# Masks of four score pairs written by ScalarE into PSUM, and a new written order for the first phase of a band-attention and feed-forward kernel

## The chip, the cores and the metric

The kernel runs on one core of one Trainium2 chip. A core has five engines, each with an instruction queue of its own that it works off strictly in order: TensorE (PE; matmuls, with weight loads shown apart as PEld), VectorE (DVE), ScalarE (ACT), GpSimd (POOL) and SyncE (SP), which only issues transfers here. ACT and POOL issue transfers too. TensorE writes its results into PSUM, eight banks of 128 x 512 fp32 numbers; DVE and ACT can read and write PSUM.

The metric is the device time of the kernel in microseconds, the median of the runs.

## The reference, cut to what matters

The inputs are q, k and v for 8 batches of 8 heads, 576 positions and 64 numbers per head, and two weight matrices, w_in of 512 x 2048 and w_out of 2048 x 512. What is computed:

```
scores = q @ k.T / sqrt(64)
mask   = (rel >= 0) & (rel < 64)            # rel = query position - key position
attn   = softmax(where(mask, scores, -1e9))
x      = (attn @ v) as 4608 rows of 512      # 8 heads side by side
h      = x @ w_in
out    = max(0.01 * h, h) @ w_out
```

All of it is fp32.

## The kernel before, in words

**Attention.** A query block of 64 positions sees only its own 64 keys and the 64 before. Two such query blocks make a pair m, 36 pairs in all; a pair's scores fill two PSUM banks (j = 0 and 1), with number b = 2m + j. So one bank is 128 keys x 512 (four head pairs, two query blocks, 64 queries). The mask is added in PSUM: before the score matmuls, one matmul of a unit matrix with the mask pattern (0 or a large negative number) writes the whole bank, and the scores then accumulate on it. Softmax runs over the 128 partitions: POOL takes the maximum over them, DVE subtracts it, ACT takes the exponential, and the sum comes out of the value matmul through a column of ones beside v.

**Feed-forward.** fp32 weights and activations are split into a high and a low part of a faster format (fp32r in the profile), and each product is three matmuls. The weights arrive as 64-bit numbers in 32 raw blocks (w_in and w_out by turns), and DVE and ACT turn each into fp32 and then into the two parts.

**Stages.** The 4608 rows are 9 chunks of 512. A first phase does attention for pairs 0 to 7 (chunks 0 and 1) and most of the feed-forward products of these chunks, while the weights are converted. It follows a list written out by hand, ORDER (line 54): every name in it is one step, the list is walked once, and each engine's queue gets its instructions in just this order. What stands behind the bar in ORDER, and all later stages (the rest of the attention, then products for the other chunks that use seven in place of eight block products), is ordered by a planner with fixed costs; the planner does not look at the first phase.

The steps of ORDER, by their letters, with the engine and the line of the profile:

| step | what it does | engine, line |
|---|---|---|
| q, k, v (number m) | loads of a pair | SP, 163, 167, 174 |
| raw n | loads weight block n (n < 3 on SP, else on ACT) into one of three buffers | 210 |
| bits, sign, clamp, join, rest n | conversion of weight block n | DVE, 225, 229, 237, 242, 251 |
| abs, chi n | conversion of weight block n; chi also stores the block of w_in | ACT, 233, 245 |
| X n | n idle matmuls on zeros | PE, 503 |
| S m | mask matmuls (312) and score matmuls (278) of pair m | PE |
| Z b | mask of pair 0, added behind its scores | PE, 312 |
| E b | scores out of PSUM: b < 2 on DVE (322), else on ACT (324) | |
| P b | maximum over the partitions | POOL, 332 |
| N b | subtracts the maximum by a matmul in the bank, b < 4 | PE, 346 |
| sub b | subtracts the maximum, b from 4 | DVE, 337 |
| exp b | exponential | ACT, 351, 353 |
| V b | values | PE, 367 |
| sm, rec, y b | sum, its inverse, the product | DVE, 374, 379, 386 |
| T m | transposes the pair's result into a PSUM bank | PE, 393 |
| H m, L m | high and low part of x | ACT 397, DVE 401 |
| M k | first product of job k, 12 matmuls | PE, 431 |
| lk, gh, gl k | leaky ReLU and the two parts of its result | ACT 436, 441, DVE 445 |
| W k | second product of job k | PE, 467 |
| ev | an accumulated bank out of PSUM | ACT, 476 |

Jobs 0 to 5 take half of chunk 0 each (256 columns; jobs 0 to 2 need x of pairs 0 and 1, jobs 3 to 5 of pairs 2 and 3), jobs 6 to 10 the whole of chunk 0, jobs 11 to 18 chunk 1. M k needs the L of its pairs and the rest of its weight block; W k needs gl k.

The banks: scores of pairs 1 and 3 use two banks of one pool (tags o0, o1); those of the other pairs use tags s and t, and so does T from pair 2 on (tag s). T of pairs 0 and 1 uses tag o3.

Of the kernel before, what the change touches and what calls it, by code (L numbers as in the profile page):

```python
# [60 lines left out]
E9 S5 v5 q6 k6 raw8 lk3 gh3 chi5 abs6 sub8 bits7 exp8 gl3 M4 lk4 rest5 sign7 clamp6 W2 V8 P9 abs7 sub9 join6 gh4 raw9  # L61
M5 bits8 gl4 E10 sm8 sign8 exp9 chi6 W3 P10 clamp7 rec8 y8 join7 rest6 lk5 abs8 clamp8 gh5 V9 M6 W4 gl5 join8 bits9
sub10 sm9 sign9 rec9 y9 raw10 E11 raw11 chi7 P11 chi8 lk6 exp10 T4 gh6 abs9 rest8 rest7 bits10 M7 V10 W5 gl6 sign10
clamp9 H4 abs10 sub11 join9 L4 bits11 sm10 rec10 clamp10 y10 join10 lk7 raw12 exp11 gh7 gl7 S6 V11 chi9 rest9 sign11
# [40 lines left out]
def band_attention_ffn(ctx: ExitStack, tc: tile.TileContext, qk, vW, vL, w_in, w_out, eye_mask, out, outT):  # L105
# [159 lines left out]

    def quarter_scores(m, ps, begun, more=False):

        q = q_of(m)  # L270
# [1156 lines left out]
```

## Time and profile before

| what | value |
|---|---|
| median of three runs | 850.16 us (849.91 to 851.41) |
| the profiled execution's own time | 850.4 us |
| its span, first to last instruction | 848.6 us |
| PE busy | 841.8 us, 99% |
| weight loads busy | 686.3 us, 81% |
| DVE busy | 620.1 us, 73% |
| ACT busy | 375.7 us, 44% |
| POOL busy | 383.3 us, 45% |
| data moved | 226.80 MB, 267 GB/s over the span |

An engine's busy time is the union of its instructions' times. Matmuls are pipelined, and their ends are modelled in the profile, so a matmul's own duration is longer than the step to the next one; the steps tell what a matmul costs. The same holds, less so, for DVE and ACT: an instruction's duration reaches a little into the next one.

The first phase goes to about 128.65 us, where the first product behind ORDER starts (line 920).

### The profile page before, as it was taken

The page shows a single profiled execution, that of the slowest core. Times are in us where ns is not written, and L with a number is a line of the kernel's source. Part 1 is how long each engine was busy: PE and PEld are TensorE (multiplying, and loading weights), DVE is VectorE, ACT ScalarE, POOL GpSimd, SP SyncE. Part 2 cuts the span into 40 slices and gives each one's busy share as a digit, 9 for nine tenths or more (in the row PEclk, how much of TensorE's full clock was granted, in tenths as well). Part 3 has the DMA queues.
Part 4 walks back from the last instruction along what each step waited for, and adds up shares of the span by engine and source line. Part 5 has one row for each costly group of instructions (what it writes and reads, how often), then busy time and mean ns, then how long its engine had stood idle before and what let it go on. Part 6 is the DMA issues. An engine that isn't in the chain of part 4 may idle for free.

```text
span 848.6 us, 16788 instructions
## 1 busy us (share of the span) xinstructions
PE 841.8 (99%) x6778; PEld 686.3 (81%) x6778; DVE 620.1 (73%) x883; ACT 375.7 (44%) x605; POOL 383.3 (45%) x218
## 2 busy tenths in 40 slices
...
GB/s 324 273 233 155 253 162 235 264 284 271 288 307 323 301 212 286 314 305 317 333 351 358 365 351 318 365 310 311 242 272 235 238 248 196 198 198 198 193 211 92
DMA packets 127757, 226.80 MB, mean 267 GB/s; under 512 B 15552, under 2 KB 46400, under 8 KB 127680
## 3 DMA queue, kind: packets, MB, share of 16 engines
...
## 4 chain that ended last, share of the span: by engine, by line
PE 97%; DVE 2%; DMA 0%; ACT 0%; issue 0%; ACTq 0%
PE m L1118 27%; PE z L1181 18%; PE acc L929 11%; PE h L920 11%; PE y L1138 10%; PE h L431 5%; PE acc L467 5%; PE s L278 4%; PE o L740 4%; PE o L367 1%; DMA qk<-qk 0%; PE t L393 0%; DVE raw L225 0%; PE s L312 0%; DVE w L242 0%; DVE raw L229 0%
## 5 line engine op out<-in xcount | busy, mean ns | idle before, releaser
L1118 PE MATMUL m<-pfew,p 128*128 128x512 f32 x720 | 169.4, 391 | 0.0
L1118 PEld LDWEIGHTS m<-pfew,p 128*128 128x128 f32 x720 | 134.5, 188 | 28.3
L1102 POOL DMA_DIRECT2D p<-w_first x42 | 31.8, 757 | 113.4 <-PE m L1118 61.0
L929 PE MATMUL acc<-p,gs 128*128 128x512 f32 x324 | 80.6, 394 | 0.0
L1127 DVE TENSOR_TENSOR p<-m,pxa 128x512 f32<-128x512 f32 x60 | 41.3, 689 | 47.0 <-PE m L1118 46.0
L681 POOL PARTITION_ALL_REDUCE g<-late_f x20 | 36.8, 1875 | 78.7 <-DVE late_f L666 72.0
L684 POOL PARTITION_ALL_REDUCE late_o<-late_f x20 | 66.1, 3329 | 12.2 <-ACT late_f L692 7.0
L1118 PE MATMUL m<-pxb,p 128*128 128x512 f32 x288 | 70.9, 391 | 0.0
L1130 ACT ACTIVATE p<-p 128x512 f32<-128x512 f32 x60 | 37.9, 631 | 73.6 <-DVE p L1127 73.5
L929 PEld LDWEIGHTS acc<-p,gs 128*128 128x128 f32 x324 | 59.8, 188 | 12.8
L1127 DVE TENSOR_TENSOR pxa<-m,pxa 128x512 f32<-128x512 f32 x60 | 41.4, 690 | 35.4 <-PE m L1118 34.7
L684 POOL PARTITION_ALL_REDUCE late_o<-e x18 | 59.5, 3336 | 8.5 <-ACT e L692 3.6
L1118 PEld LDWEIGHTS m<-pxb,p 128*128 128x128 f32 x288 | 53.7, 188 | 11.3
L684 POOL PARTITION_ALL_REDUCE late_o<-late_e x18 | 59.3, 3322 | 5.5 <-ACT late_e L692 5.2
L1181 PE MATMUL z<-gs,p 128*128 128x512 f32 x240 | 57.6, 389 | 0.0
L920 PE MATMUL h<-pxa,p 128*128 128x512 f32 x228 | 54.9, 390 | 0.0
L1102 POOL DMA_DIRECT2D p<-w_second x28 | 22.7, 811 | 68.5 <-PE z L1181 31.0
L1181 PEld LDWEIGHTS z<-gs,p 128*128 128x128 f32 x240 | 45.0, 188 | 9.4
L1181 PE MATMUL z<-third,p 128*128 128x512 f32 x216 | 51.9, 389 | 0.0
L1181 PE MATMUL z<-pxa,p 128*128 128x512 f32 x216 | 51.9, 389 | 0.0
L920 PEld LDWEIGHTS h<-pxa,p 128*128 128x128 f32 x228 | 42.7, 188 | 9.0
L1102 POOL DMA_DIRECT2D p<-w_sums x16 | 12.0, 747 | 80.2 <-PE z L1181 55.8
...
## 6 DMA issues: line engine op xcount, KB each, us to landing
...
```

Of the source, the lines that this page charges most:

```text
L431: nc.tensor.matmul(ps, a[:, k, :], b[:, k, part], start=n == 0, stop=n == len(terms) - 1)
L467: nc.tensor.matmul(acc[c, i], a[:, ts], b, start=begin and n == 0, stop=end and n == 2)
L681: nc.gpsimd.partition_all_reduce(most_of(j), e_of(m)[:, j], P, ReduceOp.max)
L684: nc.gpsimd.partition_all_reduce(sum_of(j), e_of(m)[:, j], P, ReduceOp.add)
L920: nc.tensor.matmul(ps, a[:, k, :], b[:, k], start=i == 0, stop=i == len(terms) - 1)
L929: nc.tensor.matmul(acc[c, i], a[:, i * P : (i + 1) * P], b, start=begin and k == 0, stop=n in ends and k == 2)
L1102: nc.gpsimd.dma_start(to, of, max_dma_last_dim=2048)
L1118: nc.tensor.matmul(tiles[b], w[:, 256 * i + 128 * kt : 256 * i + 128 * kt + 128], x_part(OF_X[k], j, kt), start=begin and c == 0, stop=c = ...
L1127: nc.vector.tensor_tensor(to(), tiles[b], x(), ALU.add)
L1130: nc.scalar.activation(to(), to() if b is None else tiles[b], AF.Prelu, alpha=0.01)
L1138: nc.tensor.matmul(tiles[i], a, b, start=f == 0 and k == 0, stop=f == FT - 1 and k == 2)
L1181: nc.tensor.matmul(tiles[b + i], a, x, start=begin and f == 0 and c == 0, stop=f == half - 1 and c == 2, skip_group_check=not begin,)
```

## The change

Six of the mask matmuls go from PE to ACT. For pairs 4 and 5 (both banks) and 6 and 7 (bank j = 1), a new step A m copies the mask pattern from SBUF into the bank with ScalarE, ahead of the score matmuls, which accumulate on it as they did on the mask matmul's result. Bank j = 0 of pairs 6 and 7 keeps its mask matmul. T of pairs 2 and 3 now uses tag o3 and no longer a score bank. And the whole list of the first phase, ahead of the bar, is replaced by another one with the same steps and the four steps A4 to A7; the list behind the bar is the same.

```diff
+SEEDED, TURNED_OVER = 4, 6
 ORDER = """
-q0 X6 S0 k1 raw0 q1 E0 P0 E1 bits0 sign0 raw1 v0 q2 k2 P1 X3 Z0 Z1 S1 abs0 E2 N0 exp0 X1 N1 bits1 sign1 abs1 clamp0
-join0 clamp1 V0 sm0 join1 exp1 V1 E3 S2 chi0 raw2 chi1 raw3 rec0 sm1 rec1 bits2 sign2 y1 y0 P2 P3 N2 raw4 E4 rest1
-rest0 E5 exp2 N3 exp3 T0 v1 V2 V3 k3 q3 abs2 H0 S3 v2 v3 q4 k4 sm2 P4 sub4 P5 rec2 sm3 L0 y2 rec3 clamp2 y3 exp4 V4 E6
-T1 join2 H1 sub5 sm4 bits3 rec4 L1 exp5 X4 V5 P6 raw5 chi2 sign3 abs3 E7 bits4 rest2 sub6 sm5 clamp3 rec5 y4 y5 sign4
-P7 M0 lk0 exp6 gh0 M1 abs4 gl0 T2 W0 join3 sub7 bits5 clamp4 V6 lk1 H2 exp7 raw6 L2 gh1 join4 V7 S4 chi4 raw7 chi3 gl1
-sm6 sign5 sm7 rest4 rec7 rec6 rest3 M2 E8 abs5 y7 y6 T3 bits6 sign6 W1 lk2 H3 L3 clamp5 P8 M3 gh2 gl2 join5 v4 k5 q5
...
-sign15 chi14 E15 exp14 chi13 abs15 lk9 gh9 P15 rec13 y13 V14 T6 rest14 rest13 sub15 M10 sm14 clamp15 gl9 rec14 join15
-y14 exp15 raw17 H6 chi15 V15 W9 bits16 sign16 L6 lk10 gh10 abs16 raw18 sm15 rec15 gl10 y15 T7 H7 rest15 W10 clamp16
-bits17 join16 sign17 L7 abs17 clamp17 join17 bits18 raw19 chi16 ev0 chi17 ev1 raw20 rest16 sign18 abs18 rest17 M11
...
-gh17 bits27 clamp26 gl17 sign27 join26 abs27 clamp27 join27 chi26 lk18 chi27 gh18 bits28 sign28 rest26 gl18 k8 q8 v8
-W17 q9
+q0 X3 X6 S0 E0 raw1 raw0 k1 q1 k2 bits0 q2 S1 v0 sign0 k3 abs0 E1 clamp0 join0 raw2 bits1 P0 E2 E3 v1 Z0 N0 raw3 sign1
+P1 exp0 Z1 bits2 abs1 clamp1 N1 q3 sign2 V0 exp1 join1 V1 P3 S2 chi0 sm0 rest0 N3 abs2 rec0 raw4 sm1 y0 clamp2 rec1 P2
+y1 N2 join2 T0 chi1 E4 exp3 exp2 rest1 X1 bits3 sign3 V3 V2 q4 P4 sub4 sm2 sm3 E5 H0 rec2 L0 y2 A4 rec3 exp4 v2 S3
+bits4 chi2 y3 V4 abs3 P5 sub5 E6 T1 H1 exp5 sign4 clamp3 L1 join3 sm4 P6 V5 sm5 sub6 raw5 M0 rec5 abs4 E7 v3 rec4 chi3
+k4 exp6 raw6 y4 rest3 S4 rest2 lk0 V6 y5 clamp4 M1 P7 gh0 v4 sub7 q5 E8 gl0 exp7 join4 bits5 sign5 raw7 chi4 P8 T2 V7
+sm6 lk1 sm7 abs5 W0 rec6 y6 sub8 H2 rest4 bits6 rec7 L2 gh1 X4 y7 M2 clamp5 E9 exp8 join5 A5 T3 H3 gl1 sign6 k5 V8 sm8
+S5 bits7 W1 raw8 chi5 rec8 abs6 lk2 sign7 abs7 P9 gh2 L3 sub9 y8 exp9 gl2 E10 clamp6 M3 V9 lk3 clamp7 join6 q7 M4 sm9
...
+bits15 E15 rest13 lk9 v7 sm13 exp14 rest14 P15 k8 rec13 sign15 W8 gh9 y13 bits16 abs15 sign16 sub15 V14 abs16 T6
+clamp15 bits17 sm14 M10 rec14 exp15 join15 chi15 clamp16 y14 raw18 H6 join16 gl9 raw19 q9 sign17 L6 V15 lk10 sm15
+rest15 abs17 rec15 y15 gh10 gl10 W9 clamp17 T7 join17 chi16 bits18 H7 L7 chi17 sign18 raw20 rest16 abs18 clamp18
+bits19 W10 join18 raw21 sign19 rest17 chi18 M11 bits20 sign20 lk11 abs19 clamp19 M12 gh11 M13 gl11 abs20 clamp20 ev1
+rest18 join19 ev0 lk12 bits21 sign21 v8 join20 chi19 raw22 abs21 rest19 gh12 clamp21 chi20 join21 W11 raw24 gl12 lk13
...
+W17
 |
...
-    def quarter_scores(m, ps, begun, more=False):
+    def quarter_scores(m, ps, begun, more=False, skip=()):
...
-                            stop=not begun and not more or (w, p) == (UNITS - 1, NP - 1),
+                            stop=not begun and not more or (w, p) == (UNITS - 1, NP - 1), skip_group_check=j in skip,
...
     def scores(m):
-        if m in (1, 3):
-            ps = [ps_o.tile([P, 512], F32, tag=f"o{j}", name=f"s{m}_{j}") for j in range(2)]
-        else:
-            ps = [bank(t, f"s{m}_{j}") for j, t in enumerate("st")]
-        for j in range(2):
-            probs[2 * m + j] = ps[j]
+        open_scores(m, range(2 if m < SEEDED else m >= TURNED_OVER))
         if m == 0:
-            quarter_scores(m, ps, False, True)
+            quarter_scores(m, [probs[j] for j in range(2)], False, True)
             return
-        for x in ps:
-            add_mask(m, x, True)
-        quarter_scores(m, ps, True)
+        for j in range(2 if m < SEEDED else m >= TURNED_OVER):
+            add_mask(m, probs[2 * m + j], True)
+        seeded = () if m < SEEDED else range(m >= TURNED_OVER, 2)
+        quarter_scores(m, [probs[2 * m + j] for j in range(2)], True, skip=seeded)
+
+    def open_scores(m, which):
+        for j in which:
+            pool, tag = (ps_o, f"o{j}") if m in (1, 3) else (ps_e, "st"[j])
+            probs[2 * m + j] = pool.tile([P, 512], F32, tag=tag, name=f"s{m}_{j}")
+
+    def seed(m):
+        open_scores(m, range(m >= TURNED_OVER, 2))
+        a = mask_of(UNITS * m).bitcast(F32)
+        n = a.shape[1]
+        a = flat(a)[:, None, :].broadcast_to([P, H // n, n * QB])
+        for j in range(m >= TURNED_OVER, 2):
+            nc.scalar.copy(probs[2 * m + j].rearrange("a (b c) -> a b c", c=n * QB), a)
...
-        pool, tag = (ps_o, "o3") if m < 2 else (ps_e, "s")
+        pool, tag = (ps_o, "o3") if m < 4 else (ps_e, "s")
...
-        S=scores, E=shield, Z=lambda b: add_mask(0, banks[b], False), P=top, N=take, sub=minus, exp=exps, V=values_q, sm=total, rec=inverse, y=product, T=turn, H=high_x, L=low_x,
+        A=seed, S=scores, E=shield, Z=lambda b: add_mask(0, banks[b], False), P=top, N=take, sub=minus, exp=exps, V=values_q, sm=total, rec=inverse, y=product, T=turn, H=high_x, L=low_x,
```

More of the change, by code (lines that the diff above doesn't have):

```diff
@@ L60 @@
-sm6 sign5 sm7 rest4 rec7 rec6 rest3 M2 E8 abs5 y7 y6 T3 bits6 sign6 W1 lk2 H3 L3 clamp5 P8 M3 gh2 gl2 join5 v4 k5 q5
[L61 to L64, printed above, removed]
@@ L65 @@
-W6 chi10 raw13 abs11 E13 E12 P12 rest10 sm11 bits12 clamp11 join11 rec11 y11 chi11 raw14 sign12 abs12 bits13 sign13
-clamp12 sub12 join12 M8 T5 v6 q7 v7 k7 W7 lk8 gh8 H5 exp12 abs13 chi12 raw15 gl8 P13 bits14 L5 V12 sign14 clamp13
-rest11 sub13 sm12 join13 rest12 rec12 S7 y12 E14 raw16 abs14 exp13 clamp14 join14 bits15 P14 W8 V13 M9 sub14 sm13
-sign15 chi14 E15 exp14 chi13 abs15 lk9 gh9 P15 rec13 y13 V14 T6 rest14 rest13 sub15 M10 sm14 clamp15 gl9 rec14 join15
-y14 exp15 raw17 H6 chi15 V15 W9 bits16 sign16 L6 lk10 gh10 abs16 raw18 sm15 rec15 gl10 y15 T7 H7 rest15 W10 clamp16
@@ L70 @@
-bits17 join16 sign17 L7 abs17 clamp17 join17 bits18 raw19 chi16 ev0 chi17 ev1 raw20 rest16 sign18 abs18 rest17 M11
-bits19 clamp18 M12 lk11 gh11 gl11 lk12 gh12 sign19 join18 M13 W11 M14 gl12 abs19 raw21 chi18 lk13 bits20 clamp19
-join19 chi19 raw22 sign20 rest18 rest19 W12 M15 gh13 gl13 abs20 W13 bits21 clamp20 sign21 join20 bits22 abs21 lk14
-sign22 clamp21 join21 raw23 chi20 M16 gh14 gl14 W14 rest20 raw24 abs22 clamp22 join22 chi21 raw25 bits23 rest21 sign23
-bits24 lk15 chi22 gh15 gl15 sign24 abs23 abs24 clamp23 join23 bits25 chi23 raw26 lk16 M17 W15 clamp24 sign25 rest22
@@ new lines @@
+bits4 chi2 y3 V4 abs3 P5 sub5 E6 T1 H1 exp5 sign4 clamp3 L1 join3 sm4 P6 V5 sm5 sub6 raw5 M0 rec5 abs4 E7 v3 rec4 chi3
+k4 exp6 raw6 y4 rest3 S4 rest2 lk0 V6 y5 clamp4 M1 P7 gh0 v4 sub7 q5 E8 gl0 exp7 join4 bits5 sign5 raw7 chi4 P8 T2 V7
+sm6 lk1 sm7 abs5 W0 rec6 y6 sub8 H2 rest4 bits6 rec7 L2 gh1 X4 y7 M2 clamp5 E9 exp8 join5 A5 T3 H3 gl1 sign6 k5 V8 sm8
+S5 bits7 W1 raw8 chi5 rec8 abs6 lk2 sign7 abs7 P9 gh2 L3 sub9 y8 exp9 gl2 E10 clamp6 M3 V9 lk3 clamp7 join6 q7 M4 sm9
+v5 rest5 W2 rec9 gh3 y9 T4 raw9 gl3 join7 E11 bits8 chi6 lk4 raw10 gh4 P10 sub10 H4 sign8 rest6 L4 abs8 clamp8 exp10
@@ new lines @@
+M5 q6 chi7 P11 W3 join8 V10 A6 k6 S6 bits9 sign9 gl4 sm10 raw11 rest7 lk5 v6 abs9 M6 bits10 rec10 gh5 sub11 gl5 sign10
+y10 clamp9 E12 P12 join9 bits11 exp11 raw12 V11 W4 chi8 chi9 sm11 sign11 rec11 rest8 W5 y11 lk6 abs10 sub12 gh6
+clamp10 E13 k7 rest9 M7 abs11 join10 gl6 T5 exp12 raw13 V12 clamp11 chi10 join11 lk7 P13 raw14 H5 bits12 W6 gh7 sign12
+rest10 chi11 abs12 A7 sub13 L5 gl7 sm12 clamp12 q8 join12 rest11 rec12 bits13 chi12 exp13 M8 raw15 sign13 lk8 S7 y12
+bits14 sign14 abs13 gh8 abs14 V13 W7 rest12 clamp13 join13 E14 P14 clamp14 raw16 join14 sub14 chi13 M9 gl8 chi14 raw17
```

5 lines of the change are left out of this document (4 added, 1 removed).

## The prediction

> **What bounds the kernel now.** I read first the busy times, then the chain of waits, then the stretches.
>
> ```profile
> span 848.6 us, 16788 instructions
> PE 841.8 (99%) x6778; PEld 686.3 (81%) x6778; DVE 620.1 (73%) x883; ACT 375.7 (44%) x605; POOL 383.3 (45%) x218
> ```
> ```profile
> 6.78:86.58 79.80, 78.55 (x992) 60.66 (x993) 77.58 (x167) 50.76 (x94) 31.80 (x16) 1.00 0.75 242
> 87.85:128.65 40.80, 40.80 (x182) 33.80 (x181) 34.47 (x65) 23.22 (x39) 0.00 (x0) 1.00 0.69 223
> 128.65:844.80 716.15, 716.15 (x5533) 586.98 (x5531) 505.71 (x649) 298.75 (x467) 351.34 (x198) 1.00 0.91 274
> ```
>
> The columns are stretch, length, then the busy time of PE, weight load, DVE, ACT and POOL. From 87.85 on PE never stops (40.80 of 40.80, 716.15 of 716.15). So whatever time the start of the kernel gains or loses by 87.85 arrives unchanged at the end, as long as nothing new holds PE up later. Before that the picture is different: from 6.78 to 86.58 DVE is busy 77.58 of 79.80, ACT only 50.76 of it. The chain of waits in time order (start, length, what) shows where PE takes over:
>
> ```profile
> 4.74 2.05 PE s L278 x64
> 24.50 1.64 PE h L431 x12
> 37.06 1.60 PE h L431 x12
> 57.19 0.46 PE s L312 x2
> 57.65 1.09 PE s L278 x64
> 59.35 2.99 PE acc L467 x12
> 84.67 0.44 PE t L393 x4
> 85.11 2.75 PE acc L467 x12
> 87.85 8.16 PE h L431 x36
> 128.65 1.36 PE h L920 x6
> 768.66 76.17 PE z L1181 x336
> ```
>
> These are S0, M0, M3, the masks and scores of pair 5 or later, a W, T7, W10, M11 to M13, the first product after the explicit order, and the last stage, whose 336 matmuls at 0.227 us have no gap. The first phase therefore has two limits: PE's own work behind each point, and the DVE work that has to be finished before that point. The change shifts both, so I cost both.
>
> **What PE saves.** A mask matmul is 0.23 us (two in 0.46 at 57.19). Pairs 4 and 5 lose two each, 6 and 7 one each: 6 x 0.227 = 1.36 us off PE. Scores and value products switch TensorE between two number formats, and the switches show as excess: 2.99 against 2.75 for the same twelve matmuls. In the new order S4 stands next to V6, S5 next to V8 and S7 next to V13, where S6 and V11 part; I count one round trip fewer behind M0, about 0.3 us. If PE alone set the pace, the change would be worth 1.36 + 0.3 = 1.7 us.
>
> **What ACT pays.** Six copies of 128x512 from SBUF into PSUM. The trace has none; the nearest row goes the other way, from PSUM, two in 1.08 us, so 0.54 each and 3.2 us in all.
>
> ```profile
> 6.14 0.35 ACT L517 CAST away<-p 128x192 fp32r<-128x192 f32 x1 [3.20 <-DMA p<-eye_mask]
> 132.51 0.63 ACT L245 CAST p<-w 128x512 fp32r<-128x512 f32 x1
> 133.03 1.08 ACT L476 COPY e<-acc 128x512 f32<-128x512 f32 x2
> ```
>
> The bounds are 0.35 (a cast of 192 columns) and 0.63 (a cast within SBUF), so 2.1 to 3.8 us. I take the middle row, which has the same shape and one side in PSUM, and count it as free, because ACT idles 29 of the 79.8 us quoted above. If that cover is gone, the exp behind a seed waits: A4 (two copies, 1.1 us) stands before exp4 on ACT, and V4 waits for exp4. That is the third rival.
>
> **What the new order does to DVE.** Here I need the length of one step. Start to start, from three neighbours: clamp 0.33, sign 0.60; join, rest, sub, L and a whole gl have the form of the 0.60 or 0.61 ones, bits and y cost as clamp does; rec is 0.09 and I take sm the same.
>
> ```profile
> 112.75 0.42 DVE L237 TENSOR_SCALAR raw<-raw 128x512 f32<-128x512 f32 x1
> 113.08 0.69 DVE L229 SCALAR_TENSOR_TENSOR raw<-raw 128x512 uint32<-128x512 uint32 x1
> 113.68 0.69 DVE L251 TENSOR_TENSOR p<-w,p 128x512 fp32r<-128x512 f32 x1
> 15.43 0.17 DVE L379 RECIPROCAL sm<-sm 128x4 f32<-128x4 f32 x1
> 23.45 0.66 DVE L401 TENSOR_TENSOR pxa<-t,pxa 128x512 fp32r<-128x512 f32 x1
> 36.34 0.69 DVE L401 TENSOR_TENSOR pxa<-t,pxa 128x512 fp32r<-128x512 f32 x1 [0.19 <-ACT pxa L397]
> 83.09 0.42 DVE L386 TENSOR_TENSOR y<-o,sm 128x256 f32<-128x256 f32 x1
> ```
>
> I then compare, for one DVE instruction that PE waits for, what stands ahead of it in the old and the new list:
> - L1, which M0 needs, ends at 24.1. New ahead of it: sign3, sign4, bits4, clamp3 (1.86); gone: sm4, rec4 (0.16). Later by 1.7.
> - L3, which M3 needs, ends at 37.0. New ahead: sub8, join5, sign7, clamp5, bits7, sm8, rec8. Later by 2.65.
> - y15, which T7 needs, ends at 83.5. New ahead: bits17, clamp16, join16, sign17, rest15 (2.46); gone: gl10 (0.6). Later by 1.9.
>
> So DVE does more weight work ahead of the attention steps. It is a shift, not more work: the sum over the order is unchanged.
>
> **The first 15 us.** This part starts DVE later as well.
>
> ```profile
> 0.00:10.00 10.00, 8.14 (x141) 5.77 (x141) 3.67 (x6) 2.19 (x4) 2.62 (x6) 1.00 0.82 292
> ```
> ```profile
> 1.45 2.93 PE L503 MATMUL idle<-p 128*128 128x512 f32 x6 [1.45 <-DVE p L514]
> 6.66 0.97 PE L503 MATMUL idle<-p 128*128 128x512 f32 x3
> 6.78 1.29 DVE L322 SCALAR_TENSOR_TENSOR e<-s,p 128x512 f32<-128x512 f32 x2 [5.38 <-PE s L278]
> 9.54 1.31 DVE L225 TENSOR_SCALAR raw<-raw 128x512 uint32<-128x512 uint32 x1
> 13.93 1.58 DVE L242 SCALAR_TENSOR_TENSOR w<-raw 128x512 uint32<-128x512 uint32 x1
> 15.77 0.40 DVE L225 TENSOR_SCALAR raw<-raw 128x512 uint32<-128x512 uint32 x1
> 13.92 1.78 POOL L332 PARTITION_ALL_REDUCE p<-p  x1 [0.42 <-ACT p L324]
> ```
>
> X3, which stood behind S0, moves in front of it. Six idle matmuls take 2.93 us at the start, so nine, at 0.49 each, end at 5.85, or a little before, since the last one's tail is counted in: I take 5.6, and S0 starts there and not at 4.74. S0 took 2.05 us where later scores take 1.09, and the idle matmuls at 6.66 are already fast (0.32 each), so the slow stretch ends about then: S0 from 5.6 is slow for 1.1 us, does half, and does the other half in 0.55. E0 starts near 7.3 in place of 6.78: +0.5.
>
> [...]
>
> Next, the queue of SP. In front of raw2 (third weight block) the new order puts k3.
>
> ```profile
> L210 SPq DMA_DIRECT2D raw<-w_in x1: 328/328/328, 6.1 to 6.1; - x1
> ```
> ```profile
> DMA to landing us min/median/max: 8.2/8.2/8.2
> ```
> ```profile
> 10.00:12.00 2.00, 1.88 (x16) 0.82 (x9) 1.97 (x3) 1.55 (x4) 2.00 (x2) 1.00 1.05 403
> ```
>
> raw2 landed at 6.1 + 8.2 = 14.3, and the DMA engines are full then (share 1.05, 403 GB/s); 256 KB more ahead of it make 0.65 us, so it lands between 14.3 and 15.0. Before, bits2 began at 15.77 and didn't wait. In the new order it is DVE's ninth instruction, behind sign1. Adding E0 at 7.3, then bits0, sign0, E1, clamp0, join0, bits1, sign1, 4.0 us in steps, and twice the 1.0 by which such steps are longer while POOL starts a reduction (1.31 for 0.33 at 9.54, 1.58 for 0.60 at 13.93 beside the reduction of 13.92), sign1 ends at 13.3 to 13.5. bits2 waits 0.8 to 1.5. At 14.6 DVE has then done eight of the ten instructions that it had done at 13.93; clamp1 and sm0 are missing (0.42). Behind bits2 on DVE stand clamp1, sign2, join1, sm0, and behind those T0. Lateness of DVE: 0.65 + 0.42, about 1.0 us. raw1 now goes ahead of k1 and q1, 1.3 us at that rate for the data of S1; of POOL's work only P2 and P3 hang on S1, and P0 and P1, near 2 us each, go before them. On ACT, raw3 (which waits for join0) stands before exp0; join0 ends about when N0 does, so I put nothing down; without that exp0 would be the half microsecond late that a step of DVE takes.
>
> The rest of the moved steps I cost at nothing. The loads k8, q8, v8 and q9 leave the end of SP's list for earlier places and are needed only behind the order's end at 128.65; the two evictions come later, but M11 to M13 (8.16 us) cover them, and W11 would wait up to 1.1 us without that cover.
>
> **The sum.** What stands behind each point on PE runs to 128.65.
> - By T7: y15 at 83.5 + 1.9 + 1.0 = 86.4; behind T7 nothing changes, 128.65 - 84.67 = 44.0. End of the phase 130.4: +1.7.
> - By M3: L3 at 37.0 + 2.65 + 1.0 = 40.7. Behind M3 stood 91.6; S5 (1.09), its two masks (0.45) and V8 (0.61, the gap between the scores' end at 58.74 and the W at 59.35 holds such a one) no longer stand there, and two masks of S6 and S7 (0.45) are gone: -2.6. End 129.7: +1.0.
> - By M0: L1 at 24.1 + 1.7 + 1.0 = 26.8; behind it 104.15 - 1.36 + 0.9 (X4, now behind M0) less the half microsecond that M1 waits today (row below). End 130.0: +1.4.
>
> ```profile
> PE h L431 <- ACT g L436: 0.5, 1, 0.5
> ```
> ```profile
> DVE gs L445 <- ACT gs L441: 1.2, 3, 0.6
> ```
>
> Against this stands the slack of DVE, 2.2 us from 6.78 to 86.58, of which the second row has 1.2: gl waits for ACT. With more weight work ahead of the gl the wait should shrink; it may save nothing or 2.2, and I take 0.6, half of that row. The three points give 1.0 to 1.7, on the mean 1.4, and 1.4 - 0.6 = +0.8 us. Span 849.4; the profiled run was 850.4, 1.8 around the span, so 851.2, and the median of the runs lies 0.24 below that run: **851.0 us**.
>
> **The rivals.** A measurement of this kernel tells a difference from none at about 0.2%, 1.7 us, so the forecast counts as no change.
> - *DVE catches up and PE sets the pace.* For: DVE's sum is the same, 2.2 us of it is idle. Against: the lateness sits where DVE had no gap. Gain 1.7 us, 848.5, and 0.5 more if M1's wait goes too: 848.0.
> - *Slower: DVE late at W9.* New ahead of gl9, which W9 needs, are bits16, sign16, bits17, rec14, join15, clamp16, y14, join16: 3.2 us. If no slack is won back and raw2 lands at 15.0, 0.4 later than I took, gl9 ends at 79.1 + 3.2 + 1.4 = 83.7, T7 comes a W of 2.99 later at 86.7 in place of 84.67, and all behind it is 2.1 late: 852.3. It decides from a gl9 end of 83.3 on.
>
> ```profile
> 78.45 0.69 DVE L445 TENSOR_TENSOR gs<-g,gs 128x512 fp32r<-128x512 f32 x1
> ```
>
> - *ACT is no free place.* Each seed holds the exps behind it on ACT, 3.2 us over four seeds; if the products that stand between on PE hide only half, 1.6 comes on top of the forecast: 852.6. Against: ACT's idle share.
> - *The warm-up pays.* Today PE pauses before S0; with nine idle matmuls it doesn't, and full rate may come sooner. At the earliest the first six are slow, to 4.4, and three fast ones end at 5.1, S0 at 6.2, E0 starts at 6.3, 1.0 before the forecast's: 850.0. That the change of rate came only with the matmuls of 6.66 speaks against it. [...]
>
> **Chances.** Forecast 0.36, warm-up 0.07 (both within 0.2%: 0.43); PE sets the pace 0.25 (faster); W9 0.22 and ACT 0.10 (slower, 0.32). The forecast's own range is 849.4 to 851.9; with the rivals of both signs, and leaving one in ten out at each end, 847.7 to 853.4.
>
> **What would show it.** E0 at 7.3; a DVE gap of about one microsecond before bits2; M0 near 26.8; no mask matmul on PE for pairs 4 and 5; DVE idle less than 2.2 us up to L7; M11 near 88.7 and from there no gap. I am wrong if M11 starts before 87 or after 90, or if PE shows a gap after it.

## The result, and the profile after

The changed kernel takes **858.79 us** (median of five runs, 858.43 to 860.81), the one before 850.08 beside it: a ratio of 1.0107, with a 95% interval of 1.0092 to 1.0123. The change makes the kernel 8.7 us slower, where 851.0 was forecast and 853.4 was the end of the range. The profiled run took 858.43.

The first rows are the head of the changed kernel's page and its stretches (stretch, length, busy time of PE, weight load, DVE, ACT, POOL, granted clock, DMA share, GB/s), cut at the same events as those of before: E0 to the end of L7, M11 to the first product behind the order, and the rest.

```profile
span 856.7 us, 16775 instructions
...
PE 842.4 (98%) x6772; PEld 686.5 (80%) x6772; DVE 624.5 (73%) x883; ACT 378.9 (44%) x611; POOL 384.5 (45%) x218
```
```profile
7.12:94.90 87.78, 78.88 (x984) 61.19 (x985) 84.57 (x171) 55.06 (x104) 32.90 (x16) 0.98 0.72 235
95.88:136.68 40.80, 40.80 (x182) 33.80 (x181) 33.13 (x62) 22.63 (x39) 0.00 (x0) 1.00 0.57 183
136.68:852.90 716.22, 716.17 (x5533) 587.00 (x5531) 504.63 (x650) 299.29 (x467) 351.42 (x198) 1.00 0.92 274
```

Behind M11 nothing has changed: 40.80 and 716.2 us, as before, and TensorE without a gap. The whole loss lies in front of it: M11 starts at 95.88, before at 87.85, +8.03, and the span grew by 8.1. In the stretch from E0 to L7 VectorE is busy for 84.57 us, 7.0 more than before. Three more of its instructions stand ahead of L7 in the new list (bits18, clamp17, join17), and a fourth begins just before L7 ends. It has hardly waited longer (2.4 us, before 1.6); it has been working longer.

The groups of VectorE's instructions by line and shape (count, busy us, mean ns, idle time ahead of them) say which of them take longer. Before, up to the end of L7:

```profile
L242 DVE SCALAR_TENSOR_TENSOR w<-raw 128x512 uint32<-128x512 uint32 x17 | 12.8, 751 | 0.3 <-DMA w_single<-w 0.2
...
L237 DVE TENSOR_SCALAR raw<-raw 128x512 f32<-128x512 f32 x17 | 8.2, 485 | 0.0
...
L251 DVE TENSOR_TENSOR pfew<-w,pfew 128x512 fp32r<-128x512 f32 x10 | 7.5, 763 | 0.0
```

After, likewise (join, clamp and rest, lines 242, 237 and 251 before, are now lines 243, 238 and 252):

```profile
L243 DVE SCALAR_TENSOR_TENSOR w<-raw 128x512 uint32<-128x512 uint32 x18 | 13.9, 774 | 1.8 <-DMA w_single<-w 1.5
...
L238 DVE TENSOR_SCALAR raw<-raw 128x512 f32<-128x512 f32 x18 | 11.7, 656 | 0.2 <-ACT raw L234 0.2
...
L252 DVE TENSOR_TENSOR pfew<-w,pfew 128x512 fp32r<-128x512 f32 x10 | 8.9, 894 | 0.0
```

A clamp takes 656 ns in place of 485, a rest 894 in place of 763: the same instruction on the same data. The timeline shows where. First a place of the kernel before, with the reduction of P7 (start, length, engine, line):

```profile
26.74 1.88 POOL L332 PARTITION_ALL_REDUCE g<-e  x1 [1.64 <-DVE sm L374]
```
```profile
26.99 0.71 DVE L386 TENSOR_TENSOR y<-o,sm 128x256 f32<-128x256 f32 x2
27.63 0.80 DVE L229 SCALAR_TENSOR_TENSOR raw<-raw 128x512 uint32<-128x512 uint32 x1
```

Then three reductions of the changed kernel, and what VectorE does right behind their starts:

```profile
26.51 2.29 POOL L342 PARTITION_ALL_REDUCE g<-e  x1 [1.37 <-DVE e L347]
...
33.85 1.81 POOL L342 PARTITION_ALL_REDUCE g<-e  x1 [1.84 <-DVE e L347]
...
50.85 2.08 POOL L342 PARTITION_ALL_REDUCE g<-e  x1 [2.39 <-DVE e L347]
```
```profile
26.87 1.26 DVE L238 TENSOR_SCALAR raw<-raw 128x512 f32<-128x512 f32 x1
...
33.95 1.53 DVE L243 SCALAR_TENSOR_TENSOR w<-raw 128x512 uint32<-128x512 uint32 x1
...
51.20 1.53 DVE L252 TENSOR_TENSOR pfew<-w,pfew 128x512 fp32r<-128x512 f32 x1
...
54.69 0.69 DVE L243 SCALAR_TENSOR_TENSOR w<-raw 128x512 uint32<-128x512 uint32 x1 [1.02 <-DMA w_single<-w]
```

Before, two products y, which read PSUM, followed P7's start and were not touched (0.71 us for both). After, clamp3, join4 and rest6, which read only SBUF, follow the starts of P6, P8 and P11 and take 1.26, 1.53 and 1.53 us; undisturbed, these steps take 0.42, 0.69 and 0.68. I call the excess over these lengths the lengthening (counted where it is over 0.12 us). From E0 to L7 it sums to 6.7 us before and 12.1 after.

The changed kernel's chain of waits (start, length, what) tells how VectorE's lateness reached TensorE:

```profile
47.29 7.31 DMA w_single<-w
54.69 0.69 DVE w L243
...
57.34 4.42 PE h L441 x12
...
95.88 8.16 PE h L441 x36
```

and ScalarE's timeline at that place:

```profile
52.92 0.59 ACT L315 COPY s<-away 128x512 f32<-128x512 f32 x1
...
56.90 0.39 ACT L446 ACTIVATE g<-h 128x256 f32<-128x256 f32 x1 [3.39 <-DVE sm L384]
```

The step that set the end is M6, at 57.34. It needs the bank that lk5 empties; lk5 (56.90) writes the one tile that gl4 reads, and gl4 was VectorE's step just ahead of the sm named in the row. In front of gl4 stand join8, which waited for a store, and all the lengthening so far. From M6 on TensorE is nearly without a gap up to M11. M6 itself took 4.42 us; before, this shape took 3.02.

What TensorE lost shows in its busy time (the first number behind the length) by stretches: before from E0 to M0, then after from E0 to M0 and from M0 to M6.

```profile
6.78:24.43 17.65, 16.91 (x320) 10.89 (x321) 17.48 (x36) 10.47 (x19) 12.72 (x7) 1.00 1.02 360
```
```profile
7.12:28.27 21.15, 15.15 (x313) 9.84 (x313) 20.82 (x37) 13.19 (x25) 13.16 (x7) 1.00 0.89 304
28.27:57.34 29.07, 26.17 (x390) 21.25 (x386) 27.84 (x60) 17.96 (x37) 10.40 (x6) 0.99 0.73 239
```

It stood for 6.0 us ahead of M0, where it had stood for 0.7, and for 2.9 us from there to M6, of which 2.2 are the wait for lk5. So it stood longer ahead of M0 by 5.3 us and from M0 to M6 by at least 2.2. About 2 us of the 5.3 cost no work: the idle products X3 and X4 ran in that stretch before and now run elsewhere.

VectorE's 8.3 us at L7 (94.90 against 86.58) split so: E0 later by 0.34; work that moved ahead of L7, in the prediction's step lengths, 1.27; lengthening 5.4; waits 0.8 (1.6 to 2.4, the store's 1.02 the largest); 0.5 in excesses too small for the count. This is VectorE's account and not TensorE's: of the 12.1 us of lengthening, 9.6 lie ahead of gl4's end, and what came behind it no longer held TensorE up.

### The profile page after: what moved, and what is told of

Read it like the earlier page. It is cut to its first block, busy times and chain, and to the rows that moved or that the text cites. A ratio compares the mean times of both kernels' runs of the same rounds, so it can differ in the third digit from the quotient of the medians.

```text
span 856.7 us, 16775 instructions
## 1 busy us (share of the span) xinstructions
PE 842.4 (98%) x6772; PEld 686.5 (80%) x6772; DVE 624.5 (73%) x883; ACT 378.9 (44%) x611; POOL 384.5 (45%) x218
## 4 chain that ended last, share of the span: by engine, by line
PE 94%; DVE 5%; DMA 1%; issue 0%; ACT 0%; ACTq 0%; DVEq 0%
PE m L1128 27%; PE z L1191 18%; PE acc L939 11%; PE h L930 10%; PE y L1148 10%; PE acc L477 5%; PE h L441 4%; PE s L279 4%; PE o L750 4%; DMA w_single<-w 1%; DVE raw L230 1%; DVE w L243 1%; DVE raw L238 1%; DVE raw L226 1%; PE idle L513 1%; DVE pfew L252 0%
## 5 line engine op out<-in xcount | busy, mean ns | idle before, releaser
L342 POOL PARTITION_ALL_REDUCE g<-e x13 | 26.9, 2073 | 50.2 <-ACT e L334 33.4
```

## The experiments

Theory 1: the new order puts steps that read only SBUF behind the starts of the reductions. Rivals: weight work ahead of attention (1), the seeds (2), the first 15 us (3), and, later, the stores (4). The times of all runs, with VectorE's sums from the profiled run of each (lengthening and waits from E0 to L7, and the time from E0's start to L7's end):

```
run                          time us   ratio to before [95%]     lengthening  waits  E0 to L7
before                       850.1                                   6.7       1.6     79.8
after                        858.79    1.0107 [1.0092, 1.0123]      12.1       2.4     87.8
e1  old order, seeds         850.03    0.9997 [0.9987, 1.0007]       7.5       0.8     79.4
e2  new order, no seeds      860.48    1.0119 [1.0104, 1.0134]      12.0       2.7     88.0
e3  after, no P4 to P15      855.53    1.0062 [1.0047, 1.0077]       3.5       8.0     85.2
e4  before, no P4 to P15     850.32    0.9997 [0.9988, 1.0006]       3.0       5.2     80.1
e5  after, stores from high  858.72    1.0099 [1.0084, 1.0114]      13.1       0.6     86.9
e6  e3 and e5 together       852.91    1.0029 [1.0017, 1.0040]       4.0       2.4     80.4
e7  after, steps turned      857.59    1.0093 [1.0077, 1.0110]       6.7       5.7     86.8
e14 e7 and chi8 early        856.22    1.0077 [1.0060, 1.0094]       7.5       2.5     84.4
e8  before, steps turned     855.92    1.0064 [1.0049, 1.0079]       9.2       6.4     86.8
e9  after, old beginning     860.31    1.0103 [1.0088, 1.0119]      10.4       6.8     90.6
e12 e9's idle products only  860.10    1.0117 [1.0102, 1.0133]      12.0       5.4     90.8
e13 e9's loads only          861.88    1.0131 [1.0111, 1.0150]      11.5       5.7     90.4
e15 e12 with waits filled    859.01    1.0105 [1.0088, 1.0122]      12.1       3.2     88.5
e10 e7, e5 and e9 together   856.34    1.0059 [1.0043, 1.0074]       7.8       3.2     85.5
e11 e1, products first       850.02    0.9989 [0.9981, 0.9998]       5.1       2.9     79.7
```

The ratios are to runs of before on the same chip. Before took 850.1 to 851.15 there, so rows are best compared by their ratios.

**Order or seeds (e1, e2).** The changed code with the old list, and the new list without the seeds:

```diff
 e1: before's ORDER
-... gh0 M1 ... E9 S5 ... E11 raw11 ... E12 P12 ...
+... gh0 A4 M1 ... E9 A5 S5 ... E11 A6 raw11 ... E12 A7 P12 ...
 e2: after's ORDER without A4 A5 A6 A7
-SEEDED, TURNED_OVER = 4, 6
+SEEDED, TURNED_OVER = 8, 8
```

> The changed kernel's code with the list of before; the four seed steps alone are put into it (A4 behind gh0, A5 behind E9, A6 behind E11, A7 behind E12), and the transposes of pairs 2 and 3 go to bank o3 as in the changed kernel. Theory 1 (the new order puts VectorE's steps that read only SBUF right behind the starts of GpSimd's reductions, and they last longer there): the seeds cost nothing by themselves, so 849.0 to 850.6, that is 0 to 1 us under before (850.1), since up to 1.36 us of TensorE's masks go. Rival 2 (the seeds: ScalarE's copies into PSUM hold up ScalarE's queue, or the scores wait for them): 853 or more, most of the 8.7 us seen. Rivals 1 (weight steps moved ahead of attention) and 3 (the first 15 us) say 849 to 850.6 too.

> The changed kernel with its new list but without the seed steps A4 to A7: TensorE adds the masks of pairs 4 to 7 as before. Theory 1: the order alone makes the loss, so 858 to 860.5 (TensorE waits for VectorE in that stretch, so that six masks more of 0.23 us cost at most 1.4). Rival 2 (the seeds are the cause): 850 to 852. Rivals 1 and 3: 858 to 860.5, as theory 1.

The seeds in the old order: 850.03, no difference. The new order without them: 860.48. So the order alone makes the loss, and rival 2 falls. ScalarE does hide its copies (0.59 us for one, in the row above), and TensorE's 1.36 us saved don't come out even in the old order.

**Without the reductions (e3, e4).**

```diff
-        nc.gpsimd.partition_all_reduce(mx, probs[b], P, ReduceOp.max)
+        if b < OWN:
+            nc.gpsimd.partition_all_reduce(mx, probs[b], P, ReduceOp.max)
+    nc.gpsimd.memset(temps[:, 512:], 0.0)      # once, at the start
```

> The changed kernel without the reductions over partitions of pairs 2 to 7 (P4 to P15): GpSimd writes zeros once into the tile that they filled, and VectorE's subtractions read those zeros. So the maximum is left out of 12 softmax steps and nothing else; all of VectorE's, ScalarE's and TensorE's instructions stay. Theory 1: the lengthening beside P4 to P11, 5.6 us in the changed kernel's trace (0.43 + 0.63 + 0.84 + 0.54 + 0.98 + 0.60 + 0.77 + 0.85), goes, so 852.5 to 854.5. Rival 1 (weight work ahead of attention's steps): the order is the same, so 857.5 to 858.8. Rival 3 (the first 15 us, P0 to P3, which stay): 857.5 to 858.8.

> The kernel before without the reductions over partitions of pairs 2 to 7 (P4 to P15), as in the run beside it: the maximum is left out of 12 softmax steps. Theory 1: TensorE was without a gap from 33 us on, so only the 0.9 us beside P4 and P6 can come back: 848.8 to 850.1; the distance between this run and the changed kernel without the same reductions is then 3 to 5 us, against 8.7 with them. Rivals 1 and 3: 849 to 850.1 here, and the distance stays at 7.5 us or more.

855.53 is 3.3 us back, less than the 4.3 to 6.3 that I expected, and 850.32 nothing: the distance fell from 8.7 to 5.2. Theory 1 had said 3 to 5, its rivals 7.5 or more. That the maximum itself came earlier is no rival: in the changed kernel's trace VectorE has no wait for the result of a reduction. The lengthening of the changed order is nearly gone (12.1 to 3.5), but VectorE's waits rose from 2.4 to 8.0. The joins of this run (up to L7) name the largest, the stores:

```profile
L243 DVE SCALAR_TENSOR_TENSOR w<-raw 128x512 uint32<-128x512 uint32 x18 | 12.4, 686 | 5.1 <-DMA w_single<-w 4.8
```

A join writes one of two tiles, and the store of the one before last must have landed. A faster VectorE runs into that. (TensorE was slow in this trace too: M0 stands in its chain of waits with 2.86 us, before with 1.64, and 1.7 of VectorE's 8.0 us are waits for TensorE.)

**The stores (e5, e6).**

```diff
-            nc.scalar.dma_start(w_single[n // 2], singles[n])
+            nc.scalar.dma_start(w_single[n // 2], flat(parts(n)[0]).bitcast(F32) if 2 <= n < 16 else singles[n])
```

> The changed kernel with one source replaced: the stores to w_single of weight blocks 2, 4, ... 14 read the high part that ScalarE has just written and not the joined tile, so that the joined tile (two buffers) is free for VectorE's join of the second block after without waiting for the store to land. The same bytes go the same way; what is left out is the low part of those blocks in w_single. Theory 1 as the four runs left it (lengthened steps come first; the store waits stand behind them and come out only where the lengthening goes): the two waits in the changed kernel's trace, 1.02 and 0.47 us, go, 857.0 to 858.2. Rival 4 (the stores' holds are the main cause, and the reductions matter little): 852 to 855. Rival 1 (weight work ahead of attention): 858 to 859.

> The changed kernel without the reductions P4 to P15 (the maximum is left out of 12 softmax steps, zeros in its place) and with the stores of weight blocks 2 to 14 from the high part (their low part is left out of w_single). Without the reductions alone it took 855.5, and VectorE stood 2.25 and 2.59 us before join8 and join10 for stores that held the joined tile. Theory 1 with stores behind: both go and nothing of that size is left, 850.3 to 852. Rival 1 (the order of weight work itself sets the end, by TensorE's waits): 854.5 to 855.5, as the stores' waits only take the place of others. Rival 4 (stores alone): the same as the run with the reductions and these stores.

Alone, the free tile is worth nothing (858.72; 0.6 to 1.8 us were expected, and 858 to 859 was rival 1's forecast): its waits go, and a little more lengthening (13.1) takes part of their place. Without the reductions the same edit is worth 2.6 us (855.53 to 852.91). So the two limits cover each other, and rival 4 alone falls. Together they return 5.9 of the 8.7 us with the order untouched and TensorE's work ahead of each product the same; rival 1 can hold no more than the 2.6 us left. My 850.3 to 852 was too low by about a microsecond.

Where the 2.6 us lie shows in e6's stretches from E0 to M0 and from there to M11:

```profile
7.88:27.97 20.09, 15.22 (x313) 9.71 (x313) 19.78 (x38) 12.79 (x23) 7.73 (x4) 1.00 0.87 304
27.97:89.51 61.54, 61.48 (x679) 50.99 (x675) 58.55 (x135) 41.94 (x80) 0.00 (x0) 1.00 0.74 239
```

TensorE stands for 4.9 us ahead of M0 and for 0.06 us behind it. M0 starts 3.5 us later than before, M11 1.8. So once the lengthening and the stores' waits are gone, the weight work that moved ahead of attention further on holds nothing up; what is left arises ahead of M0. M6 takes 3.03 us here, so the slower M6 (4.42) is among the 5.9 us that came back.

**The order turned, nothing left out (e7, e8).**

```diff
 e7: after's ORDER (VectorE's steps alone are shown)
-rec3 bits4 y3 | clamp3 L1 | y4 rest3 rest2 y5 | rest5 rec9 y9 | rest6 L4 | rest14 rec13 sign15 y13
+rec3 y3 bits4 | L1 clamp3 | y4 y5 rest3 rest2 | rec9 y9 rest5 | L4 rest6 | rec13 y13 rest14 sign15
 e8: before's ORDER
-rec2 sm3 L0 y2 rec3 clamp2 y3 join2 | y4 y5 sign4 | y7 y6 bits6 sign6 | y8 join7 | y9 rest8 | y11 sign12 | y12 clamp14 | y13 rest14
+clamp2 join2 rec2 sm3 L0 y2 rec3 y3 | sign4 y4 y5 | bits6 sign6 y7 y6 | join7 y8 | rest8 y9 | sign12 y11 | clamp14 y12 | rest14 y13
```

> The changed kernel with seven of VectorE's steps that read PSUM (y3, L1, y5, rec9 and y9, L4, rec13 and y13) put just ahead of the SBUF-only step that followed the start of a reduction (bits4, clamp3, rest3, rest5, rest6, rest14). The same instructions, no engine's load changed. Theory 1: each of these six, now beginning 0.8 us or more behind the start, loses about 0.3 and not 0.54 to 0.85 us; 2.1 us less in front of the sixth first product, of which a part goes to store waits: 856.3 to 857.8. Rivals 1 and 4: 858.3 to 859.3, no difference, since the same work comes in front of each product.

> The kernel before with the opposite edit: at eight reductions (P5, P7, P8, P10, P11, P12, P14, P15) a step of VectorE that reads only SBUF (clamp2 and join2, sign4, bits6 and sign6, join7, rest8, sign12, clamp14, rest14) is put ahead of the steps that read PSUM. No seeds, the same instructions. Theory 1: 0.4 to 0.9 us of lengthening at each, 4 to 5 us more over VectorE's first 87 us; the last step in front of the second chunk ended 1.3 us before TensorE took it, so the end comes 1 to 3.5 us later: 851 to 853.5. Rivals 1 and 4: 850.1 to 850.6, since the places of weight work and of stores hardly change.

e7 gains 1.2 us, as expected, but its interval and the changed kernel's overlap; the trace says more than the time. The same steps behind the same reduction P6 as in the rows above:

```profile
26.21 2.29 POOL L342 PARTITION_ALL_REDUCE g<-e  x1 [1.04 <-ACT e L334]
```
```profile
26.59 0.69 DVE L411 TENSOR_TENSOR pxa<-t,pxa 128x512 fp32r<-128x512 f32 x1
27.20 0.63 DVE L238 TENSOR_SCALAR raw<-raw 128x512 f32<-128x512 f32 x1
...
65.17 0.69 DVE L243 SCALAR_TENSOR_TENSOR w<-raw 128x512 uint32<-128x512 uint32 x1 [2.34 <-DMA w_single<-w]
```

L1, from PSUM, is untouched at 0.69, and clamp3 takes 0.63 and not 1.26. The lengthening falls from 12.1 to 6.7, as in the kernel before; but the waits rise to 5.7, of which the last row is one.

e8 makes a loss in the old order without any of the change's other parts, and a larger one than expected (5.6 us and not 1 to 3.5). The reduction P10 in its timeline, and two of VectorE's steps, the second of them join7 behind P10:

```profile
50.05 2.05 POOL L332 PARTITION_ALL_REDUCE g<-e  x1 [5.07 <-ACT e L324]
```
```profile
40.44 0.69 DVE L401 TENSOR_TENSOR pxa<-t,pxa 128x512 fp32r<-128x512 f32 x1 [1.43 <-ACT pxa L397]
...
50.49 1.41 DVE L242 SCALAR_TENSOR_TENSOR w<-raw 128x512 uint32<-128x512 uint32 x1
```

join7, 0.69 us undisturbed, takes 1.41. Only 2.5 us of the loss are lengthening, though, and 4.8 are waits like that of the first row: the products y went back by a step, so that T, H and L came later, and VectorE stood for them. As a measure of the lengthening this run is not clean.

**ScalarE standing in order (e14).** In the changed kernel lk5 stood at the head of ScalarE's queue for 3.39 us, and chi8, with its store, behind it.

```diff
 e7's ORDER
-... rest7 lk5 ... chi8 chi9 ...
+... rest7 chi8 lk5 ... chi9 ...
```

> The changed kernel with the seven turned steps (857.6 alone) and ScalarE's split of block 8 (chi8, which issues the store that holds the joined tile) put ahead of lk5, behind which it stood 2.6 us or more for TensorE's sixth first product. Nothing is left out. Theory 1 with stores behind: the wait ahead of join10 (2.34 us with the turned steps alone) goes or falls under 0.5, the one ahead of join8 (1.44) stays, and the hidden half of the repair comes out: 855.3 to 857.0. If the stores' wait only stands for another (TensorE's): 857.2 to 858.0.

856.22, 1.4 us under e7, as expected (the two intervals overlap). The wait ahead of join10 is gone, and join10 meets a reduction in its place (1.53):

```profile
51.56 0.69 DVE L243 SCALAR_TENSOR_TENSOR w<-raw 128x512 uint32<-128x512 uint32 x1 [0.78 <-DMA w_single<-w]
57.49 0.69 DVE L243 SCALAR_TENSOR_TENSOR w<-raw 128x512 uint32<-128x512 uint32 x1
61.70 1.53 DVE L243 SCALAR_TENSOR_TENSOR w<-raw 128x512 uint32<-128x512 uint32 x1
```

So nine moved steps, with no work left out, return 2.6 us; all four runs lie below the fastest of the changed kernel (858.43).

**The disputed cost alone (m1).** Each probe is a marker, a reduction that waits for it, n delays from PSUM, and one step:

```diff
+        for form in (two_sources, one_float, one_word, two_words, from_psum):
+            for n in (None, 0, 1, 2, 3, 4, 5):
+                nc.vector.memset(probs_of[:, 0, :8], 0.0)
+                if n is not None:
+                    nc.gpsimd.partition_all_reduce(temps[:, 512:], probs_of[:, 0], P, ReduceOp.max)
+                for _ in range(n or 0):
+                    delay()
+                form()
+                nc.vector.tensor_copy(z[:, 0, :8], temps[:, 512:520])
```

> The disputed cost by itself: in front of the unchanged kernel before stand 35 probes. In each, VectorE writes a marker into the tile that a reduction over partitions then reads (128x512 floats, as in the kernel), runs 0 to 5 short steps from PSUM (0.33 us each) as a delay, and then one step of a kind: two SBUF sources in floats (as the subtractions and rests), one float source in SBUF (as clamp), one word source (as bits), two word sources (as join and sign), or PSUM less SBUF (as L). The first probe of each kind has no reduction. The time of the whole kernel says nothing. Theory 1, as the rows so far give it (in each reduction a hold of about 0.85 us, which begins when the step from SBUF that VectorE is then running ends, or at once if none runs; a step from SBUF that falls into it lasts until its end): the four kinds from SBUF last 0.2 to 0.9 us longer at one or two of the six delays, those that begin less than 0.9 us behind the reduction's start, and nothing longer at the others; the kind from PSUM is never longer. Against it: the same lengthening at all delays within the reduction's 2 us (a shared bandwidth), or PSUM steps lengthened too, or none longer (the excess in the kernel came from DMA).

The lengths in us, over the start of the step behind the start of the reduction:

```
                         alone   just ahead  0.06   0.54   1.00   1.46   1.91
two float sources         0.68     0.69      1.53   1.05   0.68   0.68   0.68
one float source          0.42     0.43      1.26   0.80   1.07   0.61   0.42
one word source           0.42     0.43      1.26   0.80   1.07   0.61   0.42
two word sources          0.69     0.69      1.52   1.06   0.68   0.68   0.68
PSUM and one SBUF source  0.69     0.69      0.68   0.68   0.68   0.68   0.68
```

Three of these probes in the timeline: two sources at 0.06, one float source at 1.00, PSUM at 0.06, each behind its reduction:

```profile
10.40 1.78 POOL L554 PARTITION_ALL_REDUCE g<-e  x1 [0.40 <-DVE e L552]
...
29.95 1.78 POOL L554 PARTITION_ALL_REDUCE g<-e  x1 [0.38 <-DVE e L552]
...
69.71 1.78 POOL L554 PARTITION_ALL_REDUCE g<-e  x1 [0.40 <-DVE e L552]
```
```profile
10.46 1.53 DVE L533 TENSOR_TENSOR p<-p 128x512 f32<-128x512 f32 x1
...
30.95 1.07 DVE L536 TENSOR_SCALAR p<-p 128x512 f32<-128x512 f32 x1
...
69.77 0.68 DVE L545 TENSOR_TENSOR p<-bench,p 128x512 f32<-128x512 f32 x1
```

It is a hold, not a shared bandwidth: the step at 0.06 and the one at 0.54 both end 1.59 us behind the reduction's start (10.46 + 1.53 - 10.40), as if begun at 0.91. Nothing from PSUM is longer (0.68 at each delay, 0.69 alone). That part of theory 1 stands in numbers. What it had not said: the kinds with one source (clamp, bits) meet a second hold, to 1.65 us (30.95 + 1.07 - 0.42 - 29.95). The step is not held until the reduction ends: the first hold is over 0.91 us behind its start, and the reduction took 1.78.

**The first 15 us (e9, e12, e13, e15).**

```diff
 e9: after's ORDER, both edits; e12 the X3 alone, e13 the loads alone
-q0 X3 X6 S0 E0 raw1 raw0 k1 q1 k2 bits0 q2 S1 v0 sign0 ... P1 exp0
+q0 X6 S0 k1 raw0 q1 E0 raw1 v0 q2 k2 bits0 S1 sign0 ... P1 X3 exp0
 e15: e12's ORDER
-... E6 T1 H1 ... P6 V5 sm5 ...
+... E6 X1 T1 H1 ... P6 X3 V5 sm5 ...
```

> The changed kernel with the first loads and idle products as before: X3 stands behind P1 again, and the loads go q0, k1, raw0, q1, raw1, v0, q2, k2 (changed kernel: q0, raw1, raw0, k1, q1, k2, q2, v0). In the six traces with the new beginning VectorE's first step E0 began at 6.99 to 8.00 us (mean 7.6), in the four with the old one at 6.40 to 6.78 (mean 6.6). Rival 3 as a part (the beginning costs 1.0 us and it reaches the end whole): E0 at 6.4 to 6.8 and 857.3 to 858.2. If the beginning is hidden: E0 early, 858.4 to 859.3.

> The changed kernel with one step moved: the three idle products X3 behind P1, as before; the loads stay in the new order. With both undone the kernel took 860.3, 1.5 us more than the changed kernel, though E0 began at 6.5 us; in that trace M0 took 2.93 us (1.70 where TensorE runs at its full rate) and the scores behind it 1.9 in place of 1.1. If it is the idle products (fewer ahead of the first scores leave TensorE at its half rate later): 859.8 to 861, M0 over 2.5 us. If it is the loads: 858.2 to 859.2.

> The changed kernel with the first loads alone in the order of before (q0, k1, raw0, q1, raw1, v0, q2, k2); X3 stays ahead of S0. If the loads are what cost 1.5 us in the run with both undone: 859.8 to 861, with VectorE's first weight step later. If it was the idle products, and the loads' order is what holds E0 up: E0 at 6.9 us or before, 857.5 to 858.6.

> The kernel with X3 behind P1 (860.1 us, granted clock 0.83 from 24 to 28 us and 0.50 from 28 to 32, 0.90, 0.50 and 0.72 from 55 to 66) with four idle products more, which fill TensorE's waits ahead of the first M0: one ahead of T1, three ahead of V5. Nothing else. Theory of the clock (TensorE's waits of 1.04, 0.48 and 1.20 us in 3.5 us drop its granted clock, and that makes M0 take 2.93 and the next scores 1.99 us): clock 1.00 from 28 to 32 us, M0 1.7, scores 1.16, some 2.0 us at that place; 857.5 to 859.2, since VectorE's lateness covers a part. If the half rate comes from elsewhere: M0 still over 2.5 us, 859.8 to 861.

E0 came early in e9 (6.53), and the time hardly fell, if at all: its ratio is 1.0103, the changed kernel's 1.0107. That speaks for the reading by which the beginning is hidden. The expectations of e12 and e13 take e9 for 1.5 us slower, from the times alone; by the ratios it was not. Neither half is faster than the changed kernel, and their intervals overlap with its own (1.0117 and 1.0131; 861.88 lies above both ranges put down for e13). What the three traces share is a TensorE that runs slowly at M0 (2.93 us in e9; 2.86 in the chains of waits of e12 and e13, where before has 1.64); in e12 M6 took 5.49. Each trace is of a run with the lowest mean clock among its four (0.992, 0.990 and 0.992; the highest are 0.998, 0.998 and 0.997). Its timeline in e12 ahead of M0:

```profile
24.49 0.69 PE L377 MATMUL o<-v,e 128*64 128x65 f32 x16 [1.03 <-DVE sm L389]
25.65 0.66 PE L403 MATMUL t<-unit,y 128*128 128x128 f32 x4 [0.48 <-DVE y L396]
27.51 1.14 PE L377 MATMUL o<-v,e 128*64 128x65 f32 x16 [1.20 <-ACT e L363]
```

and the stretches of e12 around M0 and around M6 (the granted clock is the third number from the end):

```profile
24.00:28.00 4.00, 1.83 (x28) 1.49 (x30) 4.00 (x8) 3.05 (x6) 2.63 (x2) 0.83 0.81 263
28.00:32.00 4.00, 4.00 (x44) 3.65 (x46) 3.97 (x10) 2.20 (x6) 2.43 (x2) 0.50 0.70 228
...
58.00:62.00 4.00, 3.24 (x8) 2.56 (x9) 4.00 (x10) 2.25 (x5) 1.85 (x1) 0.50 0.42 150
```

and of e15, which fills TensorE's waits ahead of M0 with four idle products:

```profile
24.00:28.00 4.00, 2.73 (x32) 1.90 (x34) 4.00 (x8) 3.05 (x6) 2.63 (x2) 1.00 0.88 273
28.00:32.00 4.00, 3.88 (x108) 3.41 (x102) 3.96 (x11) 2.82 (x6) 2.57 (x2) 1.00 0.79 241
```

and of the changed kernel, which stands through the same waits ahead of M0 (1.04, 0.48 and 1.20 us):

```profile
24.00:28.00 4.00, 1.68 (x30) 1.34 (x32) 4.00 (x8) 3.07 (x6) 2.63 (x2) 1.00 0.85 257
28.00:32.00 4.00, 3.88 (x105) 3.34 (x101) 3.97 (x11) 2.74 (x6) 2.57 (x2) 1.00 0.80 248
```

In e12 the clock drops to 0.50 where M0 and the next scores run (2.93 and 1.99 us, against 1.70 and 1.16), and again at M6 (5.49). With the waits filled it is 1.00 at M0, which takes 2.07, the scores 1.16, and the kernel 859.01, 1.1 us less, as expected; but the two intervals overlap. And the changed kernel went through the same waits unfilled at a clock of 1.00 (M0 2.08). So the waits by themselves don't bring the drop about, and that filling them prevented it is not shown. What the traces show is its price: in e12 1.2 us at M0, 0.8 at the scores and 2.5 at M6, and in the changed kernel 1.4 at M6, where the clock was 0.82 from 55 to 58 us and 0.71 from 58 to 62. What tips the clock stays open: e10, with e9's beginning, took 1.69 for M0.

**Three repairs together (e10).** The edits of e7, e5 and e9.

> The changed kernel with three edits together: the seven PSUM-reading steps ahead of their SBUF-only neighbours (857.6 alone), the stores of blocks 2 to 14 from the high part (858.7 alone, no difference; the low part of those blocks is left out of w_single), and the first loads as before. In the trace with the turned steps alone VectorE stood 1.44, 2.34 and 0.66 us for stores. If lengthened steps and stores' holds are two limits that cover each other, the three together bring more than their sum: 4.4 us of waits go, some 0.8 comes back as new lengthening, 1.0 from the beginning and 1.2 from the turned steps: 852 to 854.5. If they are independent and small, as they look alone: 1.2 + 0.1 + 1.0, 856 to 857.

856.34 looks like the small, independent reading (856 to 857). But before took 851.15 on that chip, and by the ratio, 1.0059, the run is 5.0 us over before and not the 6.3 that the times alone give; that lies between the two readings, and decides for neither. The waits went down (5.7 in e7 to 3.2), but steps that came earlier met other holds (7.8).

**A version to beat both (e11).**

```diff
 e1's ORDER
-sm0 join1 exp1 V1 E3 S2 chi0 raw2 chi1 raw3 rec0 sm1 rec1 bits2 sign2 y1 y0 P2 ... rest12 rec12 S7 y12
+sm0 rec0 y0 exp1 V1 E3 S2 chi0 raw2 sm1 rec1 y1 join1 chi1 raw3 bits2 sign2 P2 ... rec12 y12 rest12 S7
```

> A version meant to beat both: the list of before with the seeds (850.0 alone), and VectorE's PSUM-reading steps rec0, y0, sm1, rec1, y1 put ahead of join1, which lost 0.89 us behind the start of P3, and rec12, y12 ahead of rest12, which lost 0.84 us behind P14. Theory 1: 0.5 to 0.9 us less in front of the first products, and TensorE hardly waits from 33 us on: 849.0 to 849.8. If what stands in front of the first products isn't the limit: 849.8 to 850.6.

850.02 against 851.15 on that chip, 0.9989 [0.9981, 0.9998]: about 0.1% faster than before, where the change is 1.1% slower. It is less than the kernel before differs between sets of runs (850.1 to 851.15), and e1, without the turned steps, took 850.03, so I claim little for it. The time lies in the second reading's range (849.8 to 850.6, the first products are not the limit), the ratio in the first one's; the run decides for neither.

## Why the prediction was wrong, point by point

- *From 87.85 on lateness arrives 1:1.* Right: +8.03 at M11, +8.1 in the span.
- *PE saves 1.7 us.* The masks are gone, and nothing of it shows in the time: in the new order TensorE waits, and in the old one e1 measures no difference. The rival "PE sets the pace" falls.
- *ACT's seeds 0.54 each, free.* Right (0.59; e1 and e2). The ACT rival falls.
- *What the new order does to DVE.* **Here the prediction failed.** It laid the steps' lengths down as constants and said "it is a shift, not more work". The lengths depend on what the step stands next to: 5.4 us more between E0 and L7. L1, forecast to end at 26.8, ended at 28.73, and the lengthening up to it was 5.9 us, against 3.8 up to L1 before. I had the row that shows it, 1.58 for 0.60 beside the reduction of 13.92, and used it only for "twice the 1.0" in the first 15 us. e3, e7 and m1 show the mechanism.
- *The shift itself (L1 +1.7, L3 +2.65, y15 +1.9).* The count was about right. In e6, without the reductions from P4 on, L1 ended at 27.50, 0.7 past the forecast, with E0 0.6 later than forecast (7.88 and not 7.3). With shift and beginning kept, e6 is 2.6 us over before, where the sum had 0.8.
- *The first 15 us, +1.0.* E0 was forecast at 7.3 and came at 7.12. The gap ahead of bits2 wasn't there: raw2 was in time, and bits2 took 1.33 us beside P2. Right in size for VectorE, wrong in kind; and taking the beginning back (e9) returned nothing that can be told from noise. The warm-up rival: S0 ran fast (1.16 us, before 1.98), but E0 came no earlier; 850.0 was far off.
- *DVE's waits shrink, -0.6.* They grew by 0.8, with a store among them that I had not costed; once VectorE is faster they are up to 8.0 (e3). I named queue neighbours of the moved loads and of gl, but not chi's store behind lk5.
- *The points M0, M3 and T7; the rival W9.* The deciding point was M6 behind gl4, through lk5's tile. W9's place was late as that rival said (gl9 ended at 89.88, past its 83.3), but its price of 2.1 us knew only the moved work, and behind M6 TensorE never waited for it.
- *What would show it.* M0 near 26.8 came at 28.27, M11 near 88.7 at 95.88, past the 90 that I named as the sign of being wrong.

Of the 8.7 us, 5.9 are shown to hang on the lengthened steps with the stores' waits behind them (e6). The slower M6 is among them. The rest arises ahead of M0, by e6's stretches; how it is shared between the later beginning and the weight steps that moved ahead of L1 was not taken apart.
